# A sparse attention and gated mixing kernel: float64 weights decoded in 8 blocks instead of 16, and the row threshold on VectorE instead of ScalarE

## The chip, the core and the metric

The kernel runs on one core of a Trainium2 chip. The metric is the time of one execution in microseconds (us) on that core. The engines work side by side, each through its own queue in order: TensorE (PE; its weight loads are shown as PEld), VectorE (DVE), ScalarE (ACT), GpSimd (POOL), and SyncE (SP), which here sends most of the DMAs. Times of single instructions come from one profiled execution.

## What is computed

For 8 batches of 8 heads, 576 positions and 64 columns per head, attention that keeps only scores close to the largest of their row; then a gated mixing of the 512 columns that the 8 heads of a batch form together.

```python
scores = scale * (q @ k.T)                          # per head, 576 x 576
thresh = max(scores, axis=-1) - tau
attn   = exp(where(scores >= thresh, scores, -1e9) - max)
x      = (attn / (sum(attn) + 1e-9)) @ v            # heads side by side: 576 x 512
gate   = sigmoid(sum_k conv_w[k] * x shifted by k)  # 5 taps along the positions
out    = (gate * (x @ w_val)) @ w_out
```

`w_val`, `w_out` (512 x 512) and `conv_w` arrive as float64. The kernel reads them as pairs of 32-bit words and makes float32 values of them on the chip.

## The kernel before

**Tiling.** A job is one pair of heads of one batch: 32 jobs, 4 to a batch. A job has 9 score tiles of 128 rows by 576 columns, 288 in all. A score tile passes through: PE multiplies q and k into PSUM (`multiply`, L556, float32 as a high and a low part); DVE takes the negated row maximum into column 0 of a small tile `nm` (`largest`, L560); ACT computes the exponentials `e` with `nm` as bias (`weigh`, L566) and then, as a second instruction on a 128x1 operand, the threshold into column 1 of `nm` (L567); DVE compares the scores with that column, multiplies by `e` and sums the rows (`keep`, L576). `keep` gives the tile's PSUM room back; there are two such rooms, and a third one early on. The rows are then divided by their sum on POOL, DVE or ACT (L606, L604, L602), after a reciprocal on DVE (L595), transposed on PE (L656), copied by ACT (L667), and multiplied with v on PE (L703).

**Gate and products.** When a job's heads are done, POOL makes the first of the five taps (L756) into a tile `pre`, DVE the other four (L763), ACT the gate. `pre` has two rooms, each for a whole batch. After the four jobs of a batch come its 192 product matmuls (L814), first with `w_val`, then with `w_out`; they are interleaved with the score tiles of the next batch. The products of the last batch are the end of the kernel.

**Decoding the weights.** `from_f64` makes float32 values of float64 words: a square on ACT (L261), five DVE instructions in a chain (L263, L265, L268, L270, L272), and an addition on POOL (L275). `Words` then splits the values into a high part (ACT, L304) and a low part (POOL, L307). Before the change this is done in 16 blocks of 128 rows by 256 columns, 8 for each weight matrix, ordered by halves of the columns. A block's words lie in one of the two `o` rooms that also carry the outputs; its values in one of two `spare` tiles; all blocks share one scratch tile `spare_m`, and each block's DVE chain begins after that of the block before.

**Order.** The order of the instructions on each queue is worked out when the kernel is built, by a planner (`op`, `carry_out`): every operation has an engine, a due time in units of score tiles, a cost, operations that it comes after, and rooms that it takes and gives. Operations marked `DVEp` and all POOL operations are planned so that no two of them run at the same time; operations marked `DVE` are not bound in that way. The planned times only fix the order: on the chip an instruction starts when its semaphores allow it.

Of the kernel before, what the change touches and what calls it, by code (L numbers as in the profile page):

```python
# [10 lines left out]
F32 = mybir.dt.float32  # L11
# [7 lines left out]
P = 128  # L19
# [7 lines left out]
def tile_thresholded_attention_gated_mix(  # L27
# [202 lines left out]
    r_spare = Rooms(const, 2, [P, DM // 2], F32, "spare")  # L230
    spare_m = const.tile([P, DM // 2], F32, name="spare_m")


    SEND = 0.56
# [15 lines left out]

    def from_f64(words, a, m, f, due, wide, after=(), takes=()):


        i32 = lambda t: t.bitcast(I32)
        hi, lo = lambda: words()[..., 1], lambda: words().bitcast(U16)[..., 1]
        least = 2.0**-15 * 1.125
        c1, c2 = (0.21, 0.345) if wide else (0.1, 0.12)
        square = op(  # L260
            "ACT", due, 0.34, 0.5, lambda: nc.scalar.square(f, hi().bitcast(F32)), after  # L261
        )
        last = op("DVEp", due, c1, c1 + 0.1, lambda: nc.vector.tensor_scalar(  # L263
            i32(m), hi(), 3, 0x3FFFFFFF, op0=ALU.logical_shift_left, op1=ALU.bitwise_and), after)
        last = op("DVEp", due, c2, c2 + 0.1, lambda: nc.vector.scalar_tensor_tensor(  # L265
            i32(a()), hi(), -(1 << 30), i32(m), op0=ALU.bitwise_and, op1=ALU.bitwise_or),
            [last], takes)
        last = op("DVEp", due, c2, c2 + 0.1, lambda: nc.vector.scalar_tensor_tensor(  # L268
            a(), f.bitcast(F32), least * least, a(), op0=ALU.is_ge, op1=ALU.mult), [last, square])
        last = op("DVEp", due, c1, c1 + 0.1, lambda: nc.vector.tensor_scalar(  # L270
            i32(m), i32(a()), -(1 << 23), None, op0=ALU.bitwise_and), [last])
        last = op("DVEp", due, c2, c2 + 0.1, lambda: nc.vector.scalar_tensor_tensor(  # L272
            f, lo(), 2.0**-36, m, op0=ALU.mult, op1=ALU.mult), [last])
        add = op("POOL", due, 0.71 if wide else 0.2, 0.8 if wide else 0.3,
                 lambda: nc.gpsimd.tensor_add(a(), a(), f.bitcast(F32)), [last])  # L275
        return last, add

    CW = DM // 2
    weights = {}

    class Words:


        def __init__(self, u, name, w, c, d0, before):
            due = u * 3.0 - 4
            hi, lo = (t[:, c, d0 : d0 + CW] for t in w_hl[name])

            def fetch():
                self.room = r_o.take()
                nc.sync.dma_start(  # L290
                    self.words(True), w.bitcast(I32)[c * P : (c + 1) * P, 2 * d0 : 2 * (d0 + CW)]
                )

            def first():
                if not hasattr(self, "a"):
                    self.a = r_spare.take()
                return self.a

            got = op("SP", due - 8, SEND, 3.5, fetch, takes=[r_o])
            self.read, whole = from_f64(  # L300
                self.words, first, spare_m, hi, due, True, [got] + before, [r_spare]
            )
            self.read.gives = [(r_o, lambda: self.room)]
            split = op("ACT", due, 0.31, 0.5, lambda: nc.scalar.copy(hi, self.a), [whole])  # L304
            weights[name, c, d0] = op(
                "POOL", due, 0.71, 0.8,
                lambda: nc.gpsimd.tensor_sub(lo, self.a, hi.bitcast(F32)), [split],  # L307
                gives=[(r_spare, lambda: self.a)],
            )

        def words(self, flat=False):
            words = self.room[:, 0 : 2 * CW].bitcast(I32)
            return words if flat else words.rearrange("p (d t) -> p d t", t=2)

    cw_raw = const.tile([P, NE * KT, 2], I32, name="cw_raw")
    cw_work = [const.tile([P, NE * KT], t, name=f"cw{i}") for i, t in enumerate((F32, F32, F32R))]
# [194 lines left out]
    class Tile:  # L511
        def __init__(self, k, t, h, qc, grp):
# [25 lines left out]
            grp.kept = op(  # L538
                "DVE", k - DUE[2], 0.74, 0.96, self.keep, after, room + ([] if i else [r_sums]),
                [(r_s, lambda: self.s), (r_e, lambda: self.e), (r_nm, lambda: self.nm)],  # L540
            )

        def multiply(self):
# [14 lines left out]
        def largest(self):  # L558
            self.nm = r_nm.take()
            nc.vector.tensor_reduce(  # L560
                self.nm[:, 0:1], self.s[:, :, :HS], axis=AX.XY, op=ALU.max, negate=True
            )

        def weigh(self):
            self.e = r_e.take()
            nc.scalar.activation(self.e, self.s[:, :, :HS], AF.Exp, bias=self.nm[:, 0:1])  # L566
            nc.scalar.activation(  # L567
                self.nm[:, 1:2], self.nm[:, 0:1], AF.Identity, bias=less, scale=-1.0
            )
# [224 lines left out]
    def products(batch, k, last, js):  # L794
# [7 lines left out]
        def product(name, e, j, moving, need, evacuate):  # L802
# [6 lines left out]
            for c in range(NE):  # L809
                for which, (wt, i) in enumerate(((hi, 0), (hi, 1), (lo, 0))):  # L810
# [5 lines left out]
                            start=n == 0, stop=n == NM - 1,  # L816
                        )

                    after = [*need[c][j][i], weights[name, c, c0 // CW * CW], *last]
# [100 lines left out]
    last, conv_ready = from_f64(  # L920
        lambda: cw_raw, lambda: cw_work[0], cw_work[1], cw_work[2], 1, False, [got_cw]
    )
    before = [last]
    u = 0
    for name, w in (("wv", w_val), ("wo", w_out)):
        for d0 in range(0, DM, CW):
            for c in range(NE):
                words = Words(u, name, w, c, d0, before)
                before = [words.read]
                u += 1  # L930
    batches = [Batch(b) for b in range(B)]
    at = 0
    for b, g, js in units:
# [67 lines left out]
```

## Time and profile before

| | |
|---|---|
| median of 3 runs | 763.82 us (763.46 to 766.15) |
| the profiled execution | 764.22 us |
| its span, first to last instruction | 762.4 us |
| outside the span | 1.8 us |
| mean granted TensorE clock | 0.991 |

A profile shows for every engine how long it was busy, what ended each wait, and the chain of work that ended last, followed back from the last instruction. A row of a group gives its line in the kernel, the engine, the operation, what it writes and reads, how often it occurs, its busy time in us and the mean duration of one in ns. Durations of neighbours overlap a little, since an engine begins an instruction before the one ahead of it has drained; the distance between two starts is what an instruction takes from its engine.

### The profile page before, as it was taken

The page shows a single profiled execution, that of the slowest core. Times are in us where ns is not written, and L with a number is a line of the kernel's source. Part 1 is how long each engine was busy: PE and PEld are TensorE (multiplying, and loading weights), DVE is VectorE, ACT ScalarE, POOL GpSimd, SP SyncE. Part 2 cuts the span into 40 slices and gives each one's busy share as a digit, 9 for nine tenths or more (in the row PEclk, how much of TensorE's full clock was granted, in tenths as well). Part 3 has the DMA queues.
Part 4 walks back from the last instruction along what each step waited for, and adds up shares of the span by engine and source line. Part 5 has one row for each costly group of instructions (what it writes and reads, how often), then busy time and mean ns, then how long its engine had stood idle before and what let it go on. Part 6 is the DMA issues. An engine that isn't in the chain of part 4 may idle for free.

```text
span 762.4 us, 15911 instructions
## 1 busy us (share of the span) xinstructions
PE 715.9 (94%) x5216; PEld 602.5 (79%) x5216; DVE 642.8 (84%) x1365; ACT 643.7 (84%) x1474; POOL 468.0 (61%) x695
## 2 busy tenths in 40 slices
PE   3778879989999999999999999999999999999997
PEld 2565657777888887888878897888888888888897
DVE  5789999999898877898799987898889988888830
ACT  5799988988988888889889888889888998988842
POOL 2566667685667646677557865775656665755231
PEclk9899999999999999999999999999999999999999
DMA  6666646456554465445455556554565566541001
GB/s 190 168 158 171 154 117 160 115 141 175 155 148 110 127 162 138 112 124 155 133 152 136 137 155 151 144 126 96 158 160 132 135 148 162 144 94 34 32 32 63
DMA packets 62130, 101.15 MB, mean 133 GB/s; under 512 B 19296, under 2 KB 19296, under 8 KB 62048
## 3 DMA queue, kind: packets, MB, share of 16 engines
q1 hardware_dynamic: 61728, 99.58, 51.1%
q8 instruction: 42, 0.69, 0.4%
q10 hardware_dynamic: 320, 0.56, 0.3%
q14 instruction: 40, 0.33, 0.1%
HBM read 35.74 MB, written 9.44 MB: 59 GB/s over the span
## 4 chain that ended last, share of the span: by engine, by line
PE 74%; DVE 11%; ACT 7%; DMA 3%; issue 2%; POOL 2%; SPq 0%; POOLq 0%; ACTq 0%; DVEq 0%
PE acc L814 23%; PE s L556 18%; PE tp L656 15%; PE acc L703 14%; PE acc L696 3%; DVE nm L560 3%; DVE pp L576 3%; ACT e L566 2%; DVE pre L763 1%; ACT T L667 1%; DMA q_r<-qT 1%; ACT pp L602 1%; ACT nm L567 1%; DVE spare L265 1%; DVE spare L268 1%
## 5 line engine op out<-in xcount | busy, mean ns | idle before, releaser
L560 DVE TENSOR_REDUCE nm<-s 128x1 f32<-128x576 f32 x277 | 205.9, 752 | 41.5 <-PE s L556 38.5
L566 ACT ACTIVATE e<-s,nm 128x576 f32<-128x576 f32 x277 | 207.4, 749 | 21.2 <-DVE nm L560 11.3
L576 DVE SCALAR_TENSOR_TENSOR pp<-s,nm,e 128x576 f32<-128x576 f32 x245 | 198.0, 811 | 23.4 <-ACT nm L567 22.1
L656 PE MATMUL tp<-ident,pp 128*128 128x128 f32 x1152 | 179.5, 277 | 12.6 <-ACT T L667 7.7
L667 ACT COPY T<-tp 128x384 f32<-128x384 f32 x384 | 174.7, 488 | 19.6 <-PE tp L656 17.9
L556 PE MATMUL s<-KH,Q 128*128 128x288 f32 x490 | 153.9, 329 | 21.0 <-DVE pp L576 9.4
L656 PEld LDWEIGHTS tp<-ident,pp 128*128 128x128 f32 x1152 | 139.0, 142 | 21.6 <-ACT T L667 11.8
L556 PE MATMUL s<-KL,Q 128*128 128x288 f32 x490 | 138.8, 298 | 0.0
L556 PEld LDWEIGHTS s<-KH,Q 128*128 128x128 f32 x490 | 93.9, 192 | 47.0 <-DVE pp L576 15.0
L606 POOL TENSOR_SCALAR pp<-pp,sums 128x576 f32<-128x576 f32 x118 | 104.6, 891 | 39.0 <-DVE sums L595 32.3
L763 DVE SCALAR_TENSOR_TENSOR pre<-xT,cw,pre 128x576 f32<-128x576 f32 x128 | 117.1, 915 | 8.7 <-POOL pre L756 8.6
L703 PE MATMUL acc<-T,v 128*64 128x256 f32 (+1 forms) x912 | 123.0, 412 | 0.0
L703 PEld LDWEIGHTS acc<-T,v 128*64 128x64 f32 x912 | 60.4, 136 | 55.5 <-issue 21.9
L593 POOL TENSOR_SCALAR sums<-sums 128x2 f32<-128x2 f32 (+1 forms) x160 | 42.7, 267 | 95.0 <-DVE pp L576 70.9
L556 PEld LDWEIGHTS s<-KL,Q 128*128 128x128 f32 x490 | 94.1, 192 | 0.0
L567 ACT ACTIVATE nm<-nm,less 128x1 f32<-128x1 f32 x288 | 85.2, 296 | 0.0
L814 PE MATMUL acc<-gl,woh 128*128 128x320 f32 (+1 forms) x256 | 78.6, 307 | 0.5 <-POOL gl L862 0.5
L814 PE MATMUL acc<-xl,wvh 128*128 128x320 f32 (+1 forms) x256 | 78.7, 308 | 0.3 <-POOL xl L747 0.3
L814 PE MATMUL acc<-xh,wvl 128*128 128x320 f32 (+1 forms) x256 | 78.5, 306 | 0.0
L814 PE MATMUL acc<-xh,wvh 128*128 128x320 f32 (+1 forms) x256 | 78.4, 306 | 0.1
L814 PE MATMUL acc<-gh,woh 128*128 128x320 f32 (+1 forms) x256 | 77.9, 304 | 0.4 <-ACT gh L855 0.4
L814 PE MATMUL acc<-gh,wol 128*128 128x320 f32 (+1 forms) x256 | 77.9, 304 | 0.0
(92 smaller groups left out, 1348.9 us busy)
## 6 DMA issues: line engine op xcount, KB each, us to landing
KH<-kh SPq DMA_DIRECT2D x124, 144.0 KB, 2.5
KL<-kl SPq DMA_DIRECT2D x124, 144.0 KB, 2.6
k_r<-kT SPq DMA_DIRECT2D x32, 320.0 KB, 3.4
v<-vs SPq DMA_DIRECT2D x32, 320.0 KB, 3.1
q_r<-qT SPq DMA_DIRECT2D x32, 288.0 KB, 3.7
outT<-o SPq DMA_DIRECT2D x32, 288.0 KB, 2.3
Q<-qh SPq DMA_DIRECT2D x62, 128.0 KB, 2.2
Q<-ql SPq DMA_DIRECT2D x62, 128.0 KB, 2.4
```

The lines of the kernel that those rows point to most:

```text
L556: nc.tensor.matmul(s[:, a, :HS], w, m, start=i == 0, stop=i == len(terms) - 1)
L560: nc.vector.tensor_reduce(self.nm[:, 0:1], self.s[:, :, :HS], axis=AX.XY, op=ALU.max, negate=True)
L566: nc.scalar.activation(self.e, self.s[:, :, :HS], AF.Exp, bias=self.nm[:, 0:1])
L567: nc.scalar.activation(self.nm[:, 1:2], self.nm[:, 0:1], AF.Identity, bias=less, scale=-1.0)
L576: nc.vector.scalar_tensor_tensor(grp.p[:, i * S : (i + 1) * S].rearrange("p (a f) -> p a f", a=2), self.s[:, :, :HS], self.nm[:, 1:2], self.e,
L593: add = op("POOL", k - 4.9, 0.28, 0.38, lambda: nc.gpsimd.tensor_scalar(sums(), sums(), 1.0, 1e-9, op0=ALU.mult, op1=ALU.add), [self.kept])
L606: nc.gpsimd.tensor_scalar(v, v, ri(i), 0.0, op0=ALU.mult, op1=ALU.add)
L656: nc.tensor.transpose(tp[:, i * P : (i + 1) * P], self.p[:, k0 : k0 + P], ident)
L667: nc.scalar.copy(T[:, c0 : c0 + n, self.off : self.off + P], tp[:, 0 : n * P].rearrange("p (c q) -> p c q", q=P),)
L703: nc.tensor.matmul(acc[hs, :w], t.v[:, c0 : c0 + D], T[:, h * NKC + c, :], start=False, stop=c == NKC - 1, skip_group_check=True,)
L763: nc.vector.scalar_tensor_tensor(cv, pair.xT[:, i + a : i + z], cw[:, g, i : i + 1], cv, op0=ALU.mult, op1=ALU.add)
L814: nc.tensor.matmul(taken[name, e, j][:, :w], wt[:, c, c0 : c0 + P], moving(c, i)[:, hs], start=n == 0, stop=n == NM - 1,)
```

## The change

Two things change.

The threshold of a score tile's rows is no longer made by ACT as a second instruction behind the exponentials (L567 is removed). A new step `lowest` makes it on DVE, by a `tensor_scalar` of 128x1 (times -1, plus `less`), into a tile `th` of its own. `nm` shrinks from two columns to one. `keep` comes after both the exponentials and the threshold. In the planner, `lowest` is marked `DVE` with a cost of 0.08, and the cost of `weigh` falls from 0.81 to 0.55.

The weights are decoded in 8 blocks of 128 rows by 512 columns, in two lanes that take turns. A lane has a tile of its own for the values and an `o` room as scratch, which it keeps until its last block. The words of both lanes lie in one of the two `pre` rooms, which is given back when the last block of each lane has been read. A block now waits for the block before last, in its own lane, instead of the block before. The products wait for a whole block of 512 columns where they waited for one of 256.

```diff
-    r_nm = Rooms(att, 4, [P, 2], F32, "nm")
+    r_nm = Rooms(att, 4, [P, 1], F32, "nm")
+    r_th = Rooms(att, 4, [P, 1], F32, "th")
...
-    def from_f64(words, a, m, f, due, wide, after=(), takes=()):
+    def from_f64(n, words, a, m, f, due, after=()):
...
-        c1, c2 = (0.21, 0.345) if wide else (0.1, 0.12)
+        c1, c2 = 0.07 + 0.00052 * n, 0.06 + 0.00112 * n
...
+    class Lane:
+        def __init__(self, i):
+            self.i, self.read, self.free = i, [], []
+            self.whole = const.tile([P, DM], F32, name=f"whole{i}")
+
+        def words(self, flat=False):
+            room = lanes_in[0].rearrange("p e s -> p (e s)").bitcast(I32)
+            words = room[:, self.i * 2 * DM : (self.i + 1) * 2 * DM]
...
+    def words_of(u, name, w, c):
+        due = u * 6.0 - 4
+        lane = lanes[u % len(lanes)]
+        hi, lo = (t[:, c, :] for t in w_hl[name])
+
+        def fetch():
+            if not lanes_in:
+                lanes_in.append(r_pre.take())
+            if u < len(lanes):
+                lane.room = r_o.take()
+            nc.sync.dma_start(lane.words(True), w.bitcast(I32)[c * P : (c + 1) * P, :])
...
+        got = op("SP", due - 8, SEND, 4.5, fetch, lane.read + pre_taken, takes + ([] if u else [r_pre]))
...
+        read, whole = from_f64(DM, lane.words, lane.a, lane.m, hi, due, [got] + lane.free)
+        split = op("ACT", due, act(DM), act(DM) + 0.18, lambda: nc.scalar.copy(hi, lane.a()), [whole])
+        done = op("POOL", due, pool2(DM), pool2(DM) + 0.1,
+                  lambda: nc.gpsimd.tensor_sub(lo, lane.a(), hi.bitcast(F32)), [split])
+        lane.read, lane.free = [read], [done]
+        weights[name, c] = done
...
-            after = [op("ACT", k - DUE[1], 0.81, 1.0, self.weigh, [largest], [r_e])]
+            after = [
+                op("DVE", k - DUE[1], 0.08, 0.25, self.lowest, [largest], [r_th]),
+                op("ACT", k - DUE[1], 0.55, 0.76, self.weigh, [largest], [r_e]),
+            ]
...
+        def lowest(self):
+            self.th = r_th.take()
+            nc.vector.tensor_scalar(self.th, self.nm, -1.0, less, op0=ALU.mult, op1=ALU.add)
...
-            nc.scalar.activation(self.e, self.s[:, :, :HS], AF.Exp, bias=self.nm[:, 0:1])
-            nc.scalar.activation(
-                self.nm[:, 1:2], self.nm[:, 0:1], AF.Identity, bias=less, scale=-1.0
-            )
+            nc.scalar.activation(self.e, self.s[:, :, :HS], AF.Exp, bias=self.nm)
...
-                self.s[:, :, :HS], self.nm[:, 1:2], self.e,
+                self.s[:, :, :HS], self.th, self.e,
...
+    op("SP", 0, 0.0, 0.0, lambda: None, [x for lane in lanes for x in lane.read],
+       gives=[(r_pre, lambda: lanes_in[0])])
```

## Rows read from the trace of the kernel before

**Rows 1.** The page: busy time of each engine, share of the span, instructions

```profile
PE 715.9 (94%) x5216; PEld 602.5 (79%) x5216; DVE 642.8 (84%) x1365; ACT 643.7 (84%) x1474; POOL 468.0 (61%) x695
```

**Rows 2.** Windows: stretch, length, busy us (instructions), clock, DMA share, GB/s

```profile
20.00:180.00 160.00, 136.40 (x914) 104.47 (x913) 149.04 (x332) 143.65 (x331) 109.77 (x162) 0.97 0.59 149
180.00:720.00 540.00, 534.22 (x4003) 458.23 (x4002) 470.31 (x985) 473.89 (x1092) 340.98 (x503) 1.00 0.53 133
```

**Rows 3.** The page: the chain that ended last, share of the span by engine

```profile
PE 74%; DVE 11%; ACT 7%; DMA 3%; issue 2%; POOL 2%; SPq 0%; POOLq 0%; ACTq 0%; DVEq 0%
```

**Rows 4.** Groups by line: count, busy us, mean ns, idle before it

```profile
L567 ACT ACTIVATE nm<-nm,less 128x1 f32<-128x1 f32 x288 | 85.2, 296 | 0.0
L595 DVE RECIPROCAL sums<-sums 128x2 f32<-128x2 f32 (+1 forms) x160 | 24.7, 156 | 8.4 <-POOL sums L593 7.8
```

**Rows 5.** Windows of L560 alone: DVE busy us and count by stage

```profile
20.00:180.00 160.00, 45.79 (x62) 0.97 0.59 149
180.00:720.00 540.00, 164.16 (x221) 1.00 0.53 133
```

**Rows 6.** Groups by line, DVE chain of the decode; last two: durations min/median/max, by form

```profile
L263 DVE TENSOR_SCALAR spare_m<-o 128x256 int32<-128x256 int32 x16 | 6.4, 403 | 0.0
L265 DVE SCALAR_TENSOR_TENSOR spare<-o,spare_m 128x256 int32<-128x256 int32 x16 | 10.4, 648 | 0.0
L268 DVE SCALAR_TENSOR_TENSOR spare<-woh,spare 128x256 f32<-128x256 f32 x8 | 4.8, 598 | 0.0
L268 DVE SCALAR_TENSOR_TENSOR spare<-wvh,spare 128x256 f32<-128x256 f32 x8 | 4.0, 500 | 0.5 <-ACT wvh L261 0.4
L270 DVE TENSOR_SCALAR spare_m<-spare 128x256 int32<-128x256 int32 x16 | 5.7, 359 | 0.1
L272 DVE SCALAR_TENSOR_TENSOR wvh<-o,spare_m 128x256 fp32r<-128x256 uint16 x8 | 3.9, 491 | 0.0
L272 DVE SCALAR_TENSOR_TENSOR woh<-o,spare_m 128x256 fp32r<-128x256 uint16 x8 | 3.3, 414 | 0.0
...
L263 DVE TENSOR_SCALAR spare_m<-o x16: 276/307/820, 18.9 to 172.2; 128x256 int32<-128x256 int32 x16
L265 DVE SCALAR_TENSOR_TENSOR spare<-o,spare_m x16: 404/502/1093, 19.5 to 174.9; 128x256 int32<-128x256 int32 x16
```

**Rows 7.** Timeline, DVE: start us, duration us; two 128x1, two of 20 columns

```profile
3.69 0.15 DVE L83 TENSOR_SCALAR sc<-tau_sb 128x1 f32<-128x1 f32 x1 [2.83 <-DMA tau_sb<-tau]
3.76 0.14 DVE L87 TENSOR_SCALAR less<-tau_sb 128x1 f32<-128x1 f32 x1
...
16.87 0.15 DVE L263 TENSOR_SCALAR cw<-cw_raw 128x20 int32<-128x20 int32 x1
17.06 0.18 DVE L265 SCALAR_TENSOR_TENSOR cw<-cw_raw,cw 128x20 int32<-128x20 int32 x1
```

**Rows 8.** Timeline, DVE and POOL at the same moment, twice

```profile
18.50 0.19 POOL L593 TENSOR_SCALAR sums<-sums 128x2 f32<-128x2 f32 x1 [2.71 <-DVE cw L268]
18.53 0.19 DVE L270 TENSOR_SCALAR cw<-cw 128x20 int32<-128x20 int32 x1
...
207.90 1.78 POOL L382 TENSOR_TENSOR ql<-q_r,qh 128x320 fp32r<-128x320 f32 x2 [0.30 <-ACT qh L376]
208.09 0.99 DVE L604 TENSOR_SCALAR pp<-pp,sums 128x576 f32<-128x576 f32 x1
```

**Rows 9.** Waits: us in total, times, longest; whole span first, then PE from 180 to 720

```profile
DVE pp L576 <- ACT nm L567: 22.1, 60, 1.1
...
PE tp L656 <- ACT T L667: 2.8, 2, 1.7
PE s L556 <- DVE pp L576: 2.0, 4, 0.9
```

**Rows 10.** First tap of batch 1; last decode instruction on DVE, first to last start

```profile
140.49 0.75 POOL L756 TENSOR_SCALAR pre<-xT,cw 128x576 f32<-128x576 f32 x1
...
L272 DVE SCALAR_TENSOR_TENSOR woh<-o,spare_m x8: 407/414/421, 105.9 to 180.2; 128x256 fp32r<-128x256 uint16 x8
```

More of the change, by code (lines that the diff above doesn't have):

```diff
@@ L258, in from_f64 @@
         least = 2.0**-15 * 1.125
[L259 removed]
+        c1, c2 = 0.07 + 0.00052 * n, 0.06 + 0.00112 * n
         square = op(
[L261 removed]
+            "ACT", due, act(n), act(n) + 0.18, lambda: nc.scalar.square(f, hi().bitcast(F32)), after
         )
         last = op("DVEp", due, c1, c1 + 0.1, lambda: nc.vector.tensor_scalar(
[L264 removed]
+            i32(m()), hi(), 3, 0x3FFFFFFF, op0=ALU.logical_shift_left, op1=ALU.bitwise_and), after)
         last = op("DVEp", due, c2, c2 + 0.1, lambda: nc.vector.scalar_tensor_tensor(
[L266 to L267 removed]
+            i32(a()), hi(), -(1 << 30), i32(m()), op0=ALU.bitwise_and, op1=ALU.bitwise_or), [last])
         last = op("DVEp", due, c2, c2 + 0.1, lambda: nc.vector.scalar_tensor_tensor(
@@ L270, in from_f64 @@
         last = op("DVEp", due, c1, c1 + 0.1, lambda: nc.vector.tensor_scalar(
-            i32(m), i32(a()), -(1 << 23), None, op0=ALU.bitwise_and), [last])
+            i32(m()), i32(a()), -(1 << 23), None, op0=ALU.bitwise_and), [last])
         last = op("DVEp", due, c2, c2 + 0.1, lambda: nc.vector.scalar_tensor_tensor(
-            f, lo(), 2.0**-36, m, op0=ALU.mult, op1=ALU.mult), [last])
-        add = op("POOL", due, 0.71 if wide else 0.2, 0.8 if wide else 0.3,
+            f, lo(), 2.0**-36, m(), op0=ALU.mult, op1=ALU.mult), [last])
@@ L275, in from_f64 @@
+        add = op("POOL", due, pool2(n), pool2(n) + 0.1,
                  lambda: nc.gpsimd.tensor_add(a(), a(), f.bitcast(F32)), [last])
         return last, add
-    CW = DM // 2
     weights = {}
[L281 to L291, printed above, removed]
-                )
[L294 to L309, printed above, removed]
@@ L311, in words, with a, m @@
+    class Lane:
+        def __init__(self, i):
+            self.i, self.read, self.free = i, [], []
+            self.whole = const.tile([P, DM], F32, name=f"whole{i}")
         def words(self, flat=False):
-            words = self.room[:, 0 : 2 * CW].bitcast(I32)
+            room = lanes_in[0].rearrange("p e s -> p (e s)").bitcast(I32)
+            words = room[:, self.i * 2 * DM : (self.i + 1) * 2 * DM]
             return words if flat else words.rearrange("p (d t) -> p d t", t=2)
+        def a(self):
+            return self.whole
+        def m(self):
+            return self.room[:, 0:DM]
@@ new lines, in tile_thresholded_attention_gated_mix @@
+    lanes_in = []
+    lanes = [Lane(i) for i in range(2)]
+    def words_of(u, name, w, c):
[8 more added lines that the diff above has]
+            nc.sync.dma_start(lane.words(True), w.bitcast(I32)[c * P : (c + 1) * P, :])
+        takes = [r_o] if u < len(lanes) else []
+        got = op("SP", due - 8, SEND, 4.5, fetch, lane.read + pre_taken, takes + ([] if u else [r_pre]))
+        if not u:
+            pre_taken.append(got)
+        read, whole = from_f64(DM, lane.words, lane.a, lane.m, hi, due, [got] + lane.free)
[4 more added lines that the diff above has]
+        weights[name, c] = done
+        if u >= 2 * NE - len(lanes):
+            read.gives = [(r_o, lambda: lane.room)]
@@ L315, in tile_thresholded_attention_gated_mix @@
+    pre_taken = []
     cw_raw = const.tile([P, NE * KT, 2], I32, name="cw_raw")
@@ L817, in run @@
                         )
-                    after = [*need[c][j][i], weights[name, c, c0 // CW * CW], *last]
+                    after = [*need[c][j][i], weights[name, c], *last]
                     cost = 0.147 if j == 0 else 0.118
@@ L919, in tile_thresholded_attention_gated_mix @@
     got_cw = op("SP", -20, 0.1, 5.0, lambda: None)
-    last, conv_ready = from_f64(
-        lambda: cw_raw, lambda: cw_work[0], cw_work[1], cw_work[2], 1, False, [got_cw]
-    )
[L923 to L930, printed above, removed]
+    _, conv_ready = from_f64(
+        NE * KT, lambda: cw_raw, lambda: cw_work[0], lambda: cw_work[1], cw_work[2], 1, [got_cw]
+    )
+    blocks = [(name, w, c) for name, w in (("wv", w_val), ("wo", w_out)) for c in range(NE)]
+    for u, (name, w, c) in enumerate(blocks):
+        words_of(u, name, w, c)
+    op("SP", 0, 0.0, 0.0, lambda: None, [x for lane in lanes for x in lane.read],
+       gives=[(r_pre, lambda: lanes_in[0])])
     batches = [Batch(b) for b in range(B)]
```

7 lines of the change are left out of this document (2 added, 5 removed).

## The prediction, on record before the run

> **What bounds the kernel now.** I read the page's engine totals first: PE 94%, DVE 84%, ACT 84%, POOL 61% of the span [rows 1]. Such shares are averages, so the second view is the windows by stage, and they tell two stages apart [rows 2]. From 20 to 180 us DVE is busy 149.04 of 160 us (93%), ACT 143.65 (90%), PE 136.40, and PE issues 914 matmuls, 5.7 per us. From 180 to 720 us PE is busy 534.22 of 540 us with 4003 matmuls, 7.4 per us, while DVE stands at 87% and ACT at 88%. So the early stage is set by DVE, with ACT close behind, because the decode of the weights lies there and few product matmuls can be given to PE yet; later PE sets the time. The chain that ended last says the same: 74% of it lies on PE, 11% on DVE, 7% on ACT [rows 3]. What follows for any edit: a us taken from DVE before 180 us comes off the end, since the matmuls that remain start that much sooner; a us taken from DVE or ACT after it is worth only what PE waits for them. Of PE's waits from 180 to 720 us the two longest, for ACT's copies and for `keep`, are 2.8 and 2.0 us [rows 9].
>
> **The change, part by part.** *The threshold leaves ACT.* 288 instructions of 296 ns go, 85.2 us in all [rows 4]. One belongs to each score tile, and the row maximum shows where the tiles lie: 62 from 20 to 180 us, 221 from 180 to 720 us [rows 5]. That is 18.4 and 65.4 us of ACT. ACT is not what ends last in either stage, so this counts nothing directly. What depends on it: `keep` no longer stands behind the second ACT instruction. It waited for that 60 times, 22.1 us [rows 9]; that is idle time of DVE, mostly under a full PE, and most of it stays, since `keep` still has to wait for the exponentials. And T is copied sooner; I book half of PE's 2.8 us and half of its 2.0 us, 2.4 us, as gain. Without that cover of a full PE nothing more would be lost, so the bounds of this part are 0 and 4.8 us.
>
> *The threshold comes to DVE.* The trace has no such instruction between score tiles, so I bound it. From below: two `tensor_scalar` of 128x1 at the start of the kernel begin 0.07 us apart [rows 7]. From above: two instructions of 20 columns, the second of which needs the result of the first, begin 0.19 us apart [rows 7]; so much it takes where DVE has nothing to put between the maximum and the threshold. The nearest row is the reciprocal, 156 ns long [rows 4], whose end overlaps with what follows. I take 0.10, nearer to the lower end, since DVE has other tiles' work ready in a stage where it is 93% busy. From 20 to 180 us: 62 x 0.10 = 6.2 us (4.3 to 11.8). After 180 us: 221 x 0.10 = 22 us, in 540 - 470.31 = 69.7 us of DVE's idle time [rows 2, 5]; free, as PE covers it. If that cover were gone, all 22 us would count. The new wait is on DVE itself: the threshold waits for the maximum, and behind it in DVE's queue stand taps and other tiles' `keep`; PE waits for a `keep` through its PSUM room.
>
> *The decode in 8 blocks.* The five DVE instructions of a block take 6.4 + 10.4 + 4.8 + 4.0 + 5.7 + 3.9 + 3.3 = 38.5 us over 16 blocks [rows 6]. Undisturbed, the two `tensor_scalar` take 276 ns and the three others 404 ns [rows 6]: 2 x 0.276 + 3 x 0.404 = 1.76 us a block, 28.2 us for 16. The other 10.3 us are delay, 0.13 us for each of 80 instructions. For 512 columns I go by size: from 20 to 256 columns a `tensor_scalar` grows from 0.15 to 0.276 us and the other form from 0.18 to 0.404 [rows 6, 7], which is 0.53 and 0.95 ns per column, so 0.41 and 0.65 us. A block is then 2 x 0.41 + 3 x 0.65 = 2.77 us, eight are 22.2 us, and 40 delays of 0.13 add 5.2 us: 27.4 us. DVE gains 38.5 - 27.4 = 11.1 us in the early stage; between 6.0 us (if each delay doubles with the size) and 16.3 us (if the delays vanish).
>
> *The rest* I cost at nothing. ACT's squares and casts and POOL's additions and subtractions halve in number and double in size; POOL has 50 us free in the early stage [rows 2]. SP sends 8 loads instead of 16; a lane's load goes out when its last block has been read, while the other lane is decoded, and a late load leaves DVE with score tiles to do. The products need four whole blocks where they needed four halves. That costs nothing if the decode ends sooner than now, at 180.2 us [rows 10]; if not, see the third rival.
>
> *The sum*, against the profiled execution (764.22 us, 0.4 us above the median of the runs): early stage 6.2 - 11.1 = -4.9 us, later stage -2.4 us: 764.2 - 4.9 - 2.4 = 756.9 us. Its bounds: 764.2 + 4.3 - 16.3 - 4.8 = 747.4 us, and 764.2 + 11.8 - 6.0 = 770.0 us.
>
> **The rivals.** *Threshold locked out by POOL (slower).* The trace shows that some DVE instructions wait until a running POOL instruction has ended. The same 256-column `tensor_scalar` takes 276 to 820 ns [rows 6]. At 208.09 us a division on DVE begins 0.19 us after two POOL subtractions, and takes 0.99 us [rows 8]. A 20-column one at 18.53 us, with POOL busy until 18.69 us, ends at 18.72 us and takes 0.19 us, where its like takes 0.15 us alone [rows 7, 8]. `lowest` is a `tensor_scalar` too, placed without regard to POOL. If it is held in the same way, the price is the share of time that POOL is busy, 109.77 / 160 = 0.69, times what is left of its instruction. That is half of a mean one (109.77 / 162 = 0.68 us [rows 2]) less some 0.12 us of the threshold's own 0.15 us that pass meanwhile: 0.69 x 0.22 = 0.15 us. With the long ones (1.78 us for two [rows 8]) it is 0.69 x 0.44 = 0.31 us. I take 0.20. Early: 62 x 0.20 = 12.4 us more, so the early stage becomes 7.5 us longer. Later: 221 x 0.30 = 66 us of new DVE work against 69.7 us of idle time; PE then begins to wait for `keep`, and I put a tenth of it, 6.6 us, on the path in place of the gain. Time: 764.2 + 7.5 + 6.6 = 778 us (with 0.15 and nothing lost later, 769 us). It decides from the point where DVE has no idle time left: early it has 11 us, so about 0.18 us per tile. For it: DVE's small instruction of the same kind ended with POOL's. Against it: that one had 20 columns, no row has a single column beside a busy POOL, and a wait behind the maximum runs in parallel with the exponentials.
>
> [...]
>
> *Nothing that counts.* If the early stage is held by the tile's chain of PE, DVE, ACT and DVE rather than by the sum of DVE's work, and POOL holds only some thresholds, gain and loss cancel: 764 us, 761 to 767.
>
> *The words' room (slower).* The lanes hold one of the two `pre` rooms until the last block has been read. Batch 1's first tap starts at 140.49 us, and the last DVE instruction of the decode at 180.2 us now [rows 10]. If the decode ended no sooner, batch 1's taps would start some 40 us late, and the job behind would wait for the attended rows' rooms: about half of the delay, 20 us, 784 us. It decides once the decode ends after 140 us. Against it: half as many instructions, and two lanes that need not wait for each other.
>
> **How the numbers follow.** What a measurement of this kernel can tell from no change is about 0.5%, 3.8 us: 760.0 and 767.6 us. Forecast 756.9 us: 0.45, of which 0.36 below 760 and 0.09 within. Threshold held by POOL: 0.34, of which 0.25 above, 0.06 within and 0.03 below, where ACT's relief outweighs it. Nothing that counts: 0.14, all but 0.02 (below) within. The words' room: 0.07, above. That makes 0.41 faster, 0.27 same, 0.32 slower. The forecast's own range is 749 to 766 us. Both signs hold much of the chance, so the whole range runs from 749 to 779 us; beyond it lie the forecast's lowest end, the worst of the second case and most of the third rival.
>
> **What the profile after would show.** ACT's busy time falls by some 85 us, DVE's by less than 11 us or rises by up to 30 us. `lowest` has a mean near 0.15 us if it is free; if POOL holds it, its maximum reaches 0.8 us and its mean 0.3 us. The decode's DVE groups total 27 us and end before 140 us. Matmuls from 20 to 180 us rise above 914. The forecast is wrong if `lowest` is stretched, if the taps of batch 1 start later than 140 us, or if the early stage has no more matmuls though DVE has less to do.

## The result, and the profile after

In the same series of runs the changed kernel takes 756.7 us (median; 756.01 to 757.72) and the kernel before 764.61 us (763.46 to 766.15): a ratio of 0.9896 [0.9876, 0.9917], 1.0% less. The forecast was 756.9 us. The total came out; of its terms several did not, and most of what follows is about those.

The head of the page of the changed kernel: the span, each engine's busy time with its share and instructions, and the chain that ended last by engine.

```profile
span 755.5 us, 16053 instructions
PE 716.9 (95%) x5216; PEld 604.8 (80%) x5216; DVE 656.4 (87%) x1590; ACT 617.3 (82%) x1204; POOL 459.0 (61%) x668
PE 78%; DVE 10%; ACT 4%; issue 3%; DMA 2%; POOL 1%; SPq 0%; POOLq 0%; ACTq 0%; DVEq 0%
```

The span is 6.9 us shorter (762.4 before). ACT is busy 26.4 us less than in [rows 1], where 85.2 us of instructions were taken from it; DVE is busy 13.6 us more. On the chain that ended last [rows 3], PE's share rises from 74% to 78%, DVE's falls from 11% to 10% and ACT's from 7% to 4%.

The windows of the two stages of the changed kernel (stretch, length, busy us and count of PE, PEld, DVE, ACT, POOL, then clock, DMA share, GB/s), beside [rows 2]:

```profile
20.00:180.00 160.00, 140.63 (x930) 110.06 (x930) 149.86 (x355) 135.93 (x260) 113.74 (x152) 0.95 0.57 148
180.00:720.00 540.00, 538.53 (x4039) 460.15 (x4036) 487.11 (x1194) 461.01 (x909) 329.27 (x487) 1.00 0.52 133
```

The count behind PE's busy time is the number to read. Every kernel here issues 5216 matmuls, so a matmul that is missing in a window has to be made up later, at 4003 / 540 = 7.4 per us. The early stage has 930 - 914 = 16 more, 2.2 us; the later one 4039 - 4003 = 36 more, 4.9 us. Together that is 7.0 us, and the span is 6.9 us shorter. This says in which stage the time was won, not by what.

The waits of PE in the later stage of the changed kernel, all there are, and the wait of `keep` over the whole span (us in total, times, longest), beside [rows 9]:

```profile
PE tp L671 <- POOL pp L621: 0.6, 1, 0.6
PE s L570 <- DVE pp L591: 0.4, 2, 0.2
...
DVE pp L591 <- ACT e L584: 12.5, 33, 1.0
```

In the kernel before, PE waited 2.8 us for the copies of T and 2.0 us for `keep` in that stage. The first is gone, the second is 0.4 us. `keep` now waits for the exponentials 33 times, 12.5 us, where it waited for ACT's second instruction 60 times, 22.1 us.

The threshold, as a row by line and as a source view (min/median/max ns, first and last start), and the decode's rows on DVE (L262 to L270):

```profile
L580 DVE TENSOR_SCALAR th<-nm,less 128x1 f32<-128x1 f32 x288 | 58.0, 207 | 1.8
L580 DVE TENSOR_SCALAR th<-nm,less x288: 190/208/218, 10.8 to 713.3; 128x1 f32<-128x1 f32 x144
...
L264 DVE SCALAR_TENSOR_TENSOR whole<-pre,o 128x512 int32<-128x512 int32 x8 | 6.7, 841 | 0.0
L262 DVE TENSOR_SCALAR o<-pre 128x512 int32<-128x512 int32 x8 | 4.4, 546 | 0.0
L268 DVE TENSOR_SCALAR o<-whole 128x512 int32<-128x512 int32 x8 | 4.0, 505 | 0.1
L270 DVE SCALAR_TENSOR_TENSOR woh<-pre,o x4: 684/687/692, 95.9 to 152.7; 128x512 fp32r<-128x512 uint16 x4
```

A threshold lasts 0.207 us, and its longest 0.218. With the three groups not shown (L266 for both matrices, 3.2 and 2.7 us; L270 for the first, 2.7 us, and for the second, 2.8 us) the decode takes DVE 26.5 us, where [rows 6] gave 38.5. It ends at 152.7 us; in [rows 10] it ended at 180.2.

One thing had moved that the diff does not name. The divisions of the rows, which the planner shares out among three engines, in the changed kernel by line (count, busy us, mean ns):

```profile
L617 ACT ACTIVATE pp<-pp,sums 128x576 f32<-128x576 f32 x111 | 86.0, 780 | 7.7 <-DVE sums L610 7.2
L617 ACT ACTIVATE pl<-pl,sums 128x576 f32<-128x576 f32 x14 | 11.0, 784 | 0.5 <-DVE sums L610 0.5
L619 DVE TENSOR_SCALAR pp<-pp,sums 128x576 f32<-128x576 f32 x31 | 19.2, 620 | 0.6
```

ACT now does 125 of them. In the kernel before it did 91 (L602), DVE 57 (now 34) and POOL 140 (now 129). The planner counts 0.26 less for each `weigh`, and gives ACT 34 divisions more, at 0.78 us some 26 us. And 85.2 us of durations were never 85.2 us of busy time, since neighbours overlap: in e4 below, 288 instructions of the same size, 86.5 us by their durations, raise ACT's busy time by 46.8 us (617.3 to 664.1). 26 - 47 = -21 us; the decode's own rows on ACT fall by 3 us more (13.5 to 10.5). The 2 us that are left of the measured 26.4 are not traced.

So part of ACT's relief reaches DVE. The divisions on DVE alone from 180 to 720 us, L604 of the kernel before and L619 of the changed one (busy us and count):

```profile
180.00:720.00 540.00, 30.52 (x48) 1.00 0.53 133
180.00:720.00 540.00, 19.89 (x32) 1.00 0.52 133
```

They take DVE 10.6 us less there, and 2.8 us less before 180 us (4.05 to 1.27).

### The profile page after: what moved, and what is told of

It is laid out like the page before. It is cut to its first block, busy times and chain, and to the rows that moved or that the text cites. A ratio compares the mean times of both kernels' runs of the same rounds, so it can differ in the third digit from the quotient of the medians.

```text
span 755.5 us, 16053 instructions
## 1 busy us (share of the span) xinstructions
PE 716.9 (95%) x5216; PEld 604.8 (80%) x5216; DVE 656.4 (87%) x1590; ACT 617.3 (82%) x1204; POOL 459.0 (61%) x668
## 4 chain that ended last, share of the span: by engine, by line
PE 78%; DVE 10%; ACT 4%; issue 3%; DMA 2%; POOL 1%; SPq 0%; POOLq 0%; ACTq 0%; DVEq 0%
PE acc L829 24%; PE s L570 19%; PE tp L671 16%; PE acc L718 14%; PE acc L711 4%; DVE pp L591 3%; DVE nm L574 3%; DVE pre L778 2%; ACT e L584 2%; PE tp L718 1%; DMA q_r<-qT 1%; ACT T L682 1%; DMA bdq<-ql 1%; DVE th L580 1%; DMA pp<-kT 0%
## 5 line engine op out<-in xcount | busy, mean ns | idle before, releaser
L591 DVE SCALAR_TENSOR_TENSOR pp<-s,th,e 128x576 f32<-128x576 f32 x245 | 198.1, 812 | 14.5 <-ACT e L584 11.6
L682 ACT COPY T<-tp 128x384 f32<-128x384 f32 x384 | 175.9, 489 | 27.3 <-PE tp L671 25.2
L671 PE MATMUL tp<-ident,pp 128*128 128x128 f32 x1152 | 184.3, 279 | 9.8 <-POOL pp L621 3.9
L570 PE MATMUL s<-KH,Q 128*128 128x288 f32 x490 | 152.4, 326 | 19.7 <-DVE pp L591 10.5
L671 PEld LDWEIGHTS tp<-ident,pp 128*128 128x128 f32 x1152 | 138.9, 142 | 20.9 <-ACT T L682 6.5
L621 POOL TENSOR_SCALAR pp<-pp,sums 128x576 f32<-128x576 f32 x114 | 97.8, 862 | 41.2 <-DVE sums L610 33.3
L608 POOL TENSOR_SCALAR sums<-sums 128x2 f32<-128x2 f32 (+1 forms) x160 | 48.1, 300 | 118.2 <-DVE pp L591 103.0
L617 ACT ACTIVATE pp<-pp,sums 128x576 f32<-128x576 f32 x111 | 86.0, 780 | 7.7 <-DVE sums L610 7.2
```

What stands on the lines that cost most here:

```text
L570: nc.tensor.matmul(s[:, a, :HS], w, m, start=i == 0, stop=i == len(terms) - 1)
L591: nc.vector.scalar_tensor_tensor(grp.p[:, i * S : (i + 1) * S].rearrange("p (a f) -> p a f", a=2), self.s[:, :, :HS], self.th, self.e, op0 ...
L608: add = op("POOL", k - 4.9, 0.28, 0.38, lambda: nc.gpsimd.tensor_scalar(sums(), sums(), 1.0, 1e-9, op0=ALU.mult, op1=ALU.add), [self.kept])
L617: nc.scalar.mul(v, v, ri(i))
L621: nc.gpsimd.tensor_scalar(v, v, ri(i), 0.0, op0=ALU.mult, op1=ALU.add)
L671: nc.tensor.transpose(tp[:, i * P : (i + 1) * P], self.p[:, k0 : k0 + P], ident)
```

## The experiments

Ratios and times are against the kernel before, run on the same chip in the same series (764.85 us for e1 to e4, 764.98 for e5 to e8, 764.56 for e9 to e12). Where a text says "against the changed kernel", its 756.7 us is meant.

### The two parts apart

e1 is the kernel before with the threshold on DVE, its planner costs included, and the old decode in 16 blocks. e2 is the changed kernel with the threshold back on ACT. e10 is e1 with the decode due sooner in the planner. Of each edit the lines that matter are shown.

```diff
# e1, against the kernel before: the threshold alone
+            nc.vector.tensor_scalar(self.th, self.nm, -1.0, less, op0=ALU.mult, op1=ALU.add)
# e2, against the changed kernel: the decode alone
-            nc.vector.tensor_scalar(self.th, self.nm, -1.0, less, op0=ALU.mult, op1=ALU.add)
+            nc.scalar.activation(
+                self.nm[:, 1:2], self.nm[:, 0:1], AF.Identity, bias=less, scale=-1.0
+            )
# e10, against e1: when a block is due
-            due = u * 3.0 - 4
+            due = u * 1.0 - 20
```

> The kernel before, with only the threshold moved to DVE (and its planner costs); the decode stays in 16 blocks. Theory A, the recorded forecast's own terms: the threshold adds 62 x 0.12 = 7.4 us of DVE work to the early stage, which DVE sets, and saves 2.4 us later, so about 769 us, no faster than before. Theory B: taking 75 to 85 us from ACT is what counts, wherever DVE still has room, and the decode counts little: 757 to 759 us, the whole gain. Theory C: neither part gains by itself, the gain is one of the order that the planner finds: 762 to 766 us here and in the next run.

> The changed kernel with the threshold put back on ACT into the second column of nm (and its planner costs); the decode stays in 8 blocks and two lanes. Theory A: DVE gains about 11 to 12 us before 180 us and that comes off the end: 752 to 754 us. Theory B: ACT is as loaded as before, so the decode alone gives 762 to 765 us. Theory C: 762 to 766 us.

> The kernel with the threshold alone on DVE and the old decode of 16 blocks, its due times pulled forward (u * 1.0 - 20 in place of u * 3.0 - 4), so that its last DVE instruction stands behind 68 row maxima in place of 80. Same work on every engine as the run with the threshold alone (768.1 us). If the late end of the decode cost that run its gain: 759 to 763 us. If DVE's added work in the early stage did: 767 to 770 us.

Measured: e1 768.12 us, ratio 1.0044 [1.0028, 1.0061]; e2 762.29 us, 0.9972 [0.9955, 0.9989] (its profiled execution is one of 760.31 us); e10 763.16 us, 0.9979 [0.9964, 0.9994]. The parts do not add: +0.4% and -0.3% apart, -1.0% together.

e1 first: its two stages, its products alone (L819) in two stretches, and the last DVE instruction of its decode.

```profile
20.00:180.00 160.00, 140.82 (x946) 109.49 (x946) 151.07 (x392) 137.72 (x277) 110.28 (x171) 0.98 0.62 155
180.00:720.00 540.00, 532.46 (x3938) 454.88 (x3937) 482.69 (x1186) 452.63 (x892) 322.34 (x480) 0.98 0.51 131
...
180.00:200.00 20.00, 0.00 (x0) 0.00 (x0) 0.66 0.63 162
200.00:220.00 20.00, 11.86 (x67) 10.80 (x67) 0.91 0.20 67
...
L273 DVE SCALAR_TENSOR_TENSOR woh<-o,spare_m x8: 403/413/418, 127.4 to 208.7; 128x256 fp32r<-128x256 uint16 x8
```

By the prediction's own steps the threshold alone gives 764.2 + 6.2 - 2.4 = 768.0 us, and 768.12 came, for another reason. The early stage is not 6.2 us late; it has 32 matmuls more than before. The new order puts score tiles ahead of the decode, whose last DVE instruction now stands behind 80 row maxima in DVE's queue (66 in the kernel before, 55 in the changed one) and starts at 208.7 us. `w_out` is not there until then, and from 180 to 200 us not one product matmul runs. The early lead is borrowed and paid back with interest: 65 matmuls fewer after 180 us.

e10 does the same work with the decode behind 68 row maxima; it ends at 187.3 us. Its stages and those of e2:

```profile
20.00:180.00 160.00, 132.41 (x880) 102.89 (x880) 149.13 (x385) 134.20 (x267) 106.71 (x162) 0.97 0.57 145
180.00:720.00 540.00, 538.89 (x4031) 459.92 (x4032) 490.74 (x1203) 461.80 (x909) 331.42 (x491) 1.00 0.52 134
...
20.00:180.00 160.00, 136.38 (x932) 107.27 (x932) 141.73 (x301) 140.49 (x314) 112.25 (x147) 0.98 0.58 145
180.00:720.00 540.00, 534.65 (x4019) 458.18 (x4020) 474.18 (x991) 476.36 (x1098) 345.37 (x508) 1.00 0.53 134
```

e10 is nearer to what the threshold does by itself: 34 matmuls fewer early (4.6 us lost), 28 more later (3.8 us won). Its decode still ends 7 us after that of the kernel before, and 12 of the 34 are product matmuls (120 early, 132 before).

e2 is what the decode does alone. The prediction's steps give it 764.2 - 11.1 = 753.1 us; it came to 762.29. The 11.1 us were a sum of durations; DVE's busy time in the early stage falls by 7.3 us, from 149.04 to 141.73, and ACT stands at 140.49. Only 18 matmuls (2.4 us) come of it. The rest of DVE's room turns into waiting, here DVE's two longest waits from 20 to 180 us in the kernel before and in e2:

```profile
DVE nm L560 <- PE s L556: 6.7, 9, 4.0
DVE pp L576 <- ACT nm L567: 1.8, 6, 0.6
...
DVE nm L570 <- PE s L566: 8.7, 12, 1.6
DVE pp L586 <- ACT nm L577: 6.5, 14, 1.3
```

DVE waits for the next scores, and `keep` waits for ACT's second instruction: over both tiles that it writes (for the other, `pl`, 1.0 and 1.9 us) 2.8 us before and 8.4 us in e2. In the changed kernel `keep` waits 3.1 us there, for the exponentials.

The early counts do not add: -34 and +18 would make -16, and the changed kernel has +16. Two things in the runs bear on this gap. `keep` no longer stands behind ACT's second instruction. And the place of the decode alone moves as many matmuls: e8 below, the changed kernel with the decode ending at 170.4 us in place of 152.7, has 898 early, 32 fewer. How much belongs to either was not separated.

### Whether POOL holds the threshold

e3 makes the same threshold in two columns in place of one, in the same order of instructions. `keep` reads the first of the two.

```diff
-    r_th = Rooms(att, 4, [P, 1], F32, "th")
+    r_th = Rooms(att, 4, [P, 2], F32, "th")
...
-            nc.vector.tensor_scalar(self.th, self.nm, -1.0, less, op0=ALU.mult, op1=ALU.add)
+            nc.vector.tensor_scalar(self.th, self.nm.to_broadcast([P, 2]), -1.0, less, op0=ALU.mult, op1=ALU.add)
```

> The changed kernel, same order of instructions, with the threshold written as two equal columns (its input column read twice). The changed kernel's own threshold takes 190 to 218 ns whether POOL is busy or not. [...] If such a small operand is not held at all, mean 0.21 us and 756 to 758 us.

Measured: 786.24 us, 1.0285 [1.0267, 1.0304]; 29.5 us above the changed kernel. e3's threshold as a row and a source view, two lines of its timeline (start us, duration us), and its stages:

```profile
L580 DVE TENSOR_SCALAR th<-nm,less 128x2 f32<-128x2 f32 x288 | 108.6, 383 | 1.7
L580 DVE TENSOR_SCALAR th<-nm,less x288: 202/229/1380, 10.8 to 742.2; 128x2 f32<-128x2 f32 x144
...
208.42 0.87 POOL L393 TENSOR_TENSOR ql<-q_r,qh 128x320 fp32r<-128x320 f32 x1
208.50 0.82 DVE L580 TENSOR_SCALAR th<-nm,less 128x2 f32<-128x2 f32 x1
...
20.00:180.00 160.00, 136.24 (x878) 104.56 (x877) 151.63 (x340) 129.89 (x247) 109.35 (x147) 0.94 0.56 142
180.00:720.00 540.00, 529.06 (x3882) 443.72 (x3882) 508.26 (x1158) 446.64 (x876) 322.50 (x480) 1.00 0.53 133
```

With two columns the threshold that starts at 208.50 us, beside a subtraction on POOL that runs until 209.29, ends at 209.32. It is one of many: 109 of the 288 last longer than 0.3 us, all of them start while a POOL instruction runs, and all end within 0.06 us of the end of one. With one column the same meeting costs nothing; the changed kernel, DVE and POOL in one stretch:

```profile
122.05 1.15 POOL L401 TENSOR_SCALAR q_r<-q_r,sc 128x576 f32<-128x576 f32 x1
122.50 0.21 DVE L580 TENSOR_SCALAR th<-nm,less 128x1 f32<-128x1 f32 x1
122.62 0.75 DVE L574 TENSOR_REDUCE nm<-s 128x1 f32<-128x576 f32 x1
```

The threshold starts under POOL's 1.15 us and is done 0.49 us before POOL is. Of the 288 starts 204 fall into a POOL instruction, 84 do not; both have a mean of 207 ns. And the next instruction starts 0.12 us after it, which is what a threshold takes from DVE (the median of all 288 is 0.13 us).

So the rival of the held threshold is real for two columns and not for one: the mean is 383 ns with two, where one column has 207 beside a busy POOL and beside an idle one. Why the number of columns decides was not shown.

e12 is the same question from the other side: the planner may put each threshold on DVE (cost 0.124) or on POOL (0.28).

```diff
-                op("DVE", k - DUE[1], 0.08, 0.25, self.lowest, [largest], [r_th]),
+                op("DVE", k - DUE[1], 0.124, 0.25, self.lowest(nc.vector), [largest], [r_th],
+                   other=[("POOL", 0.28, 0.38, self.lowest(nc.gpsimd))]),
```

> A version meant to be faster than both: the planner may give a tile's threshold to DVE (cost 0.124) or to POOL (0.28), whichever is free first; 110 of 288 go to POOL. DVE loses 110 x 0.124 = 13.6 us of work: at 0.27 us per us 753 us. [...]

Measured: 763.92 us, 0.9999 [0.998, 1.0019]. 110 thresholds go to POOL, at 312 ns; DVE's early busy time falls to 143.28 us, but the stages have 926 and 4003 matmuls, so the later stage loses all that the change had won. Why it does is not settled: in a planner's new order more than the threshold moves.

### What a us of ACT is worth

e4 puts one ACT instruction of the old threshold's size (128x1) back behind each exponential, its result unread, in the changed kernel's order. e6 does so for the tiles before the 62nd only, e7 for those from the 62nd on.

```diff
+    idle_th = const.tile([P, 1], F32, name="idle_th")
...
             nc.scalar.activation(self.e, self.s[:, :, :HS], AF.Exp, bias=self.nm)
+            nc.scalar.activation(idle_th, self.nm, AF.Identity, bias=less, scale=-1.0)
```

> The changed kernel, same order, with one more 128x1 instruction on ACT behind each tile's exponentials, into a tile that nobody reads; the threshold stays on DVE. So ACT has its old load while everything else is as in the changed kernel. Theory A: ACT is not what ends last, so 757 to 759.5 us. Theory B: ACT's relief is the gain, so most of it goes: 761 to 765 us.

> The changed kernel, same order, with the extra 128x1 ACT instruction of the earlier run on the first 62 tiles only. The extra one on all 288 tiles cost 14.9 us. Theory A (DVE alone sets the early stage): 757 us here. Theory D (ACT and DVE set the early stage together, and the product matmuls catch up nothing): a tile costs most early, 62 x 0.185 = 11 us of ACT, so 763 to 768 us here and 760 to 764 us with the later 226 tiles. Theory E (every tile costs the same): 760 us here, 768 us with the later ones.

> The changed kernel, same order, with the extra 128x1 ACT instruction on tiles 62 to 287 only. Theory A (PE is full after 180 us and covers ACT): 757 to 759 us. Theory D: 760 to 764 us. Theory E: 768 us.

Measured: e4 771.61 us, 1.0104 [1.0083, 1.0124]; e6 758.54 us, 0.9903 [0.9889, 0.9916]; e7 769.83 us, 1.0045 [1.0032, 1.0059]. Against the changed kernel that is 15 us for all, about 1 us for the early tiles (0.5 by the ratios, 1.8 by the medians), and 11 to 13 us for the later ones (by the ratios, by the medians). The early stage of e6, then e7's later stage and the longest wait of PE's weight loads there for another engine:

```profile
20.00:180.00 160.00, 137.01 (x922) 105.42 (x921) 148.06 (x353) 143.32 (x316) 113.07 (x152) 0.97 0.58 146
...
180.00:720.00 540.00, 535.51 (x3943) 448.32 (x3942) 479.58 (x1171) 487.70 (x1108) 325.80 (x483) 1.00 0.53 132
...
PEld tp L674 <- ACT T L685: 9.1, 31, 0.6
```

PE's busy time falls by 3 us, from 538.53 to 535.51, and its matmuls by 96, which are 13.0 us. A PE that is "busy 99%" can still do 2.4% more or less work. The loss comes in small pieces: the weight loads of the transposes wait for ACT's copies of T 31 times, 9.1 us (4 times, 0.8 us, in the changed kernel). So in the later stage, where the prediction gave ACT's relief 2.4 us, 226 instructions of ACT, which raise its busy time there by 26.7 us, are worth 11 to 13 us in this order. That is more work than the change took away: with the 34 divisions still on ACT, e7's later stage has it busy 487.70 us, against 473.89 in the kernel before.

In the early stage, where the prediction saw ACT "close behind", 62 of them are worth about 1 us. e6 has ACT there as busy as the kernel before (143.32 and 143.65 us) and 8 matmuls fewer than the changed kernel; e7, which is the changed kernel up to the 62nd tile, has 923, 7 fewer, so 8 is no more than such counts vary. ACT's lighter load in the early stage is not what the change gains by. (e6's extra instruction is one that `keep` does not wait for.)

### What a us of DVE is worth

e5 issues each threshold a second time into an unread tile. e11 issues three more, for the tiles before the 62nd only.

```diff
             nc.vector.tensor_scalar(self.th, self.nm, -1.0, less, op0=ALU.mult, op1=ALU.add)
+            nc.vector.tensor_scalar(idle_th, self.nm, -1.0, less, op0=ALU.mult, op1=ALU.add)
```

> The changed kernel, same order, with the threshold instruction issued twice per tile on DVE (the second into a tile that nobody reads): 288 x 0.124 = 35.7 us more DVE work, 7.7 us of it on the first 62 tiles. The recorded forecast held DVE work after 180 us to be free up to 69.7 us: then only the early part counts, 764 to 765 us. Against it: the two-column threshold added 50.6 us of DVE work and 29.5 us of time, 0.58 us per us; at that rate 777 us.

> The changed kernel, same order, with three more threshold instructions on DVE for each of the first 62 tiles (into a tile that nobody reads): 62 x 3 x 0.124 = 23.1 us of DVE work in the early stage. By the recorded step (a us of DVE before 180 us is a us at the end): 779 to 781 us. By the rate of the run with one more on all tiles (9.7 us for 35.7 us): 762 to 764 us.

Measured: e5 766.38 us, 1.0023 [1.0008, 1.0038], 9.7 us above the changed kernel; e11 783.98 us, 1.0249 [1.0226, 1.0273], 27.3 us above it. e11's timeline on DVE and its early stage, then e5's stages:

```profile
104.35 0.20 DVE L581 TENSOR_SCALAR th<-nm,less 128x1 f32<-128x1 f32 x1
104.48 0.70 DVE L583 TENSOR_SCALAR idle_th<-nm,less 128x1 f32<-128x1 f32 x3
105.09 0.75 DVE L575 TENSOR_REDUCE nm<-third 128x1 f32<-128x576 f32 x1
...
20.00:180.00 160.00, 127.66 (x752) 97.37 (x751) 152.05 (x457) 115.75 (x215) 91.15 (x128) 0.87 0.50 126
...
20.00:180.00 160.00, 139.84 (x914) 108.37 (x913) 152.71 (x415) 134.24 (x257) 112.75 (x151) 0.95 0.57 146
180.00:720.00 540.00, 537.11 (x3986) 455.53 (x3986) 508.15 (x1407) 455.95 (x898) 326.66 (x486) 1.00 0.53 133
```

Counted at the 0.12 us of a single threshold, e11's extra work would be 23 us. Its timeline shows more: the three write one tile and take 105.09 - 104.48 = 0.61 us, 0.20 us each, 38 us for 62 tiles. Of those 38 us 27.3 come through, 0.72 us per us; DVE's busy time hardly rises (152.05 us), since it was full. That DVE sets the early stage holds where it gets more to do; e2 shows less of it where it gets less.

In smaller pieces the rate is lower. In e5 the early tiles get 62 x 0.13 = 8 us of DVE, and lose 16 matmuls, 2.2 us: 0.27 us per us, a rough figure, since 7 matmuls are within what such counts vary. The 11 us of decode in e2 gave 2.4. In e3 the early tiles get 62 x 0.176 = 10.9 us and lose 52 matmuls, 7.0 us, 0.64 us per us. So the early price of a us of DVE lies between a quarter (0.13 us at a time) and near three quarters (0.61 us at a time, or held by POOL); one rate for all, as the prediction had it, does not fit.

In e5's later stage 226 x 0.13 = 29 us of DVE are added, and 53 matmuls are missing, 7.2 us. e3 agrees: its threshold grows by 176 ns, 39 us over 221 tiles, and 157 matmuls are missing, 21.2 us. DVE's work in the later stage is not free, though PE is "busy 537.11 of 540 us" in e5; it costs a quarter of a us per us, and half when it comes in long pieces.

### When the decode must be done

e8 and e9 are the changed kernel with the four blocks of `w_out` due 14 and 34 score tiles later in the planner. In e8 as it ran (the shift was 14) the last DVE instruction of the decode stands behind 63 row maxima; the positions named in the text on record for it are not those of this kernel. In e9 it stands behind 82.

```diff
-        due = u * 6.0 - 4
+        due = u * 6.0 - 4 + (34 if u >= NE else 0)
```

> The changed kernel with the due time of the four w_out blocks set 34 tiles later, so that the last DVE instruction of the decode stands behind 82 row maxima in DVE's queue; it is behind 55 in the changed kernel, 66 in the one before and 80 in the run with the threshold alone. If the end of the decode is what cost that run its gain (products with w_out cannot start, PE idles and its clock falls), the time goes to 766 to 772 us, with next to no product matmuls between 180 and 200 us. If it ended the same by DVE's load alone, this run has the load of the changed kernel and stays at 756 to 759 us.

> The run e8 moved the due times by 14 tiles, not by the 34 that its expectation names: the last DVE instruction of the decode stood behind 63 row maxima (55 in the changed kernel). Here it is 34: behind 82, as in the run with the threshold alone (80). If the late end of the decode took that run's gain (some 8 us between what its engines' loads would give, 760 us, and its 768 us), this one goes to 763 to 768 us, with hardly a product matmul between 180 and 200 us. If not, it stays within 757 to 760 us as e8 did.

Measured: e8 758.51 us, 0.9909 [0.9887, 0.9932], 1 to 2 us above the changed kernel with the decode ending at 170.4 us; e9 770.34 us, 1.0072 [1.0048, 1.0097], 13.6 us above it. e9's last decode rows, its products alone in one stretch, and POOL's first tap of batch 1 with the last read of batch 0's `pre` on DVE:

```profile
L270 DVE SCALAR_TENSOR_TENSOR woh<-pre,o x4: 664/682/689, 133.0 to 216.2; 128x512 fp32r<-128x512 uint16 x4
...
180.00:200.00 20.00, 1.00 (x3) 0.84 (x3) 0.74 0.30 75
...
159.75 0.75 POOL L771 TENSOR_SCALAR pre<-xT,cw 128x576 f32<-128x576 f32 x1
160.90 0.41 DVE L853 SCALAR_TENSOR_TENSOR g<-pre,acc 128x256 f32<-128x256 f32 x1
```

From 180 to 200 us three product matmuls run, where the changed kernel runs 50. It is e1's picture, in a kernel with lanes. e1 has no lanes and no words in `pre`, so late weights are enough to make it; and in e9 the first tap of batch 1 starts at 159.75 us, 56 us before the last block is read. It did not wait for the words' room: by then nearly all of batch 0's own room had been read.

### The experiments in one view

Matmuls in the two stages less those of the kernel before, what that gives at 7.4 per us, and the difference of the profiled spans (762.4 us before):

| | early | later | worked out | span |
|---|---|---|---|---|
| the change | +16 | +36 | -7.0 us | -6.9 us |
| e1 | +32 | -65 | +4.5 | +4.0 |
| e2 | +18 | +16 | -4.6 | -4.2 |
| e10 | -34 | +28 | +0.8 | +0.5 |
| e3 | -36 | -121 | +21.2 | +22.2 |
| e4 | +5 | -59 | +7.3 | +6.4 |
| e6 | +8 | +38 | -6.2 | -7.0 |
| e7 | +9 | -60 | +6.9 | +6.3 |
| e5 | 0 | -17 | +2.3 | +2.7 |
| e11 | -162 | +11 | +20.4 | +20.9 |
| e8 | -16 | +44 | -3.8 | -4.5 |
| e9 | -3 | -64 | +9.1 | +7.8 |
| e12 | +12 | 0 | -1.6 | -0.6 |

The count of matmuls tells within 1.3 us what each kernel takes, since what is not issued by 720 us is left for the end. PE's busy time does not. The count says where time is lost; what loses it has to come from the runs. Where the cut at 180 us falls matters, though: e8 loses 32 matmuls early against the changed kernel and wins 8 back later by nothing but the order of the decode.

No kernel run here is faster than the changed one.

## Why the prediction came out, and where its steps did not

*The threshold's price on DVE* was right: 0.12 us, booked at 0.10 between 0.07 and 0.19. "Free" stood for a mean near 0.15 us, and the mean is 0.207; but its start-to-start time is what counts, and POOL adds nothing to it. The rival with POOL (778 us) falls for one column. For two, e3 came to 786 us. There, against the kernel before, the rival's early price was too high (7.5 us booked, 36 matmuls or 4.9 us missing) and its later one, "a tenth" or 6.6 us, much too small: 121 matmuls, 16.3 us.

*The decode's price* was right as a sum of durations: 26.5 us for 27.4 booked.

*"A us taken from DVE before 180 us comes off the end"* is the step that failed. The decode's 11.1 us were booked in full; e2 shows 7.3 us less of DVE's busy time and 2.4 us off the end, and DVE waiting longer, for ACT's second instruction (8.4 us) and for scores (8.7 us). That is the mechanism of the rival *Nothing that counts*, the tile's chain through PE, DVE, ACT and DVE, at work in the early stage. The same step booked the threshold at 6.2 us lost there. With both parts 4.9 us were booked as won early, and 2.2 us came.

*"Later PE sets the time, and DVE's or ACT's work is worth only what PE waits for it"* failed on both sides. ACT's work there is worth far more than half of PE's listed waits (e7: 11 to 13 us), and DVE's 22 us were booked as free, while e5's second set of the same instructions costs 7.2 us there. The decode, booked at nothing after 180 us, has 16 of the 36 matmuls in e2. The net, 4.9 us, is just above the upper bound of 4.8 us that the prediction had set; it booked 2.4.

So the total came out by luck in part: the mis-sized terms cancel, 4.9 + 2.4 forecast, 2.2 + 4.9 found. That "ACT's busy time falls by some 85 us" was wrong (26.4): it took durations that overlap for busy time, and the planner filled ACT up with divisions, some of them from DVE. What those 34 are worth by themselves was not separated from the threshold's relief.

*The decode "ends before 140 us"* was wrong (152.7 us), and the taps of batch 1 start at 155.4 us, later than the 140 us that the prediction named as a sign of failure. Yet no price shows; PE in the changed kernel:

```profile
140.00:160.00 20.00, 19.29 (x144) 16.45 (x144) 18.66 (x46) 15.91 (x31) 16.41 (x25) 1.00 0.45 115
160.00:180.00 20.00, 19.83 (x148) 16.32 (x146) 19.55 (x45) 18.20 (x37) 15.04 (x19) 1.00 0.50 130
```

The third rival's condition was met and its time (784 us) was not. Its failing link is that batch 1 must wait for the words: in e9 it does not. In the changed kernel its first tap comes 2 us after the words' last read and 15 us later than before, yet the gate that needs the taps begins no later: DVE first reads batch 1's `pre` (L838 before, L853 now) at 209.22 us, and at 213.35 us in the kernel before. What does decide is the sentence that the prediction costed at nothing, "if the decode ends sooner than now, at 180.2 us". It is the hinge of the change: with the threshold alone the decode ends at 208.7 us, and the kernel is slower than before.

The time of *Nothing that counts* (764 us) falls with the interval. Still open: why the early counts of the two parts do not add, how much of e7's 11 to 13 us belongs to an order that was planned for a lighter ACT, and why e12 loses its later gain.

## What to carry to other kernels

A us taken from the busiest engine is not a us off the end (e2: 2.4 of 11.1). Take busy time and not a sum of durations, ask what the engine will wait for once it has room, and put the second engine's busy time in the same window beside it. Do not take PE's busy share for its work: count matmuls per window and divide by the rate, and do not book other engines' work under a "full" PE at zero (here it cost a quarter to a half of its length). When costs in a planner change, look at what it moves elsewhere, and find where in each queue the last piece of shared preparation lands (here the last block of `w_out`) before adding up instructions.

## What the runs showed of the hardware

A `tensor_scalar` of one column per partition never waited for POOL (190 to 218 ns in 288), the same one with two columns did (202 to 1380 ns, mean 383), and that column cost the kernel 29.5 us.

A late weight was followed by a lower clock of PE. In e1 PE was busy 6.83 us of the 10 us before 190 us, with 39 matmuls; from 190 to 200 us the clock granted to it was 0.50 in the mean. From 200 to 220 us it was 0.91. In e9, with 34 matmuls from 180 to 190 us, it was 0.60 in the mean; in the changed kernel, with its weights in time, it was 1.00 from 180 to 200 us. The two rows of e1:

```profile
180.00:190.00 10.00, 6.83 (x39) 5.31 (x37) 9.77 (x23) 8.56 (x18) 6.36 (x10) 0.82 0.56 141
190.00:200.00 10.00, 8.26 (x30) 6.48 (x30) 9.24 (x27) 7.12 (x14) 3.92 (x7) 0.50 0.70 184
```

In the second row PE is busier than in the first and does fewer matmuls: 8.26 / 30 = 0.28 us of busy time for each at a clock of 0.50, 6.83 / 39 = 0.18 us at 0.82.
